# Normalization and output products moved from VectorE to GpSimd in pieces placed under PSUM reads, with six more VectorE tiles

## The chip, the cores and the metric

One core of a Trainium2 chip runs the kernel; seven are idle. The metric is the device time of one execution in microseconds (us). A kernel's time is the median of its runs.

## The reference, cut to what matters

```python
B, H, S, D = 1, 32, 2048, 640;  Dh = D // H            # 20 columns per head
def reference(q, k, v, t):
    eps = 1e-6
    qn = q / (jnp.sqrt((q * q).sum(axis=-1, keepdims=True)) + eps)
    kn = k / (jnp.sqrt((k * k).sum(axis=-1, keepdims=True)) + eps)
    logits = jnp.einsum('bhqd,bhkd->bhqk', qn, kn) * t[None, :, None, None]
    attn = _softmax(logits, axis=-1)
    return jnp.einsum('bhqk,bhkd->bhqd', attn, v)
```

This is attention over 32 heads with normalized queries and keys. A head has 2048 x 2048 scores, so 134 million exponentials have to be made. They are the work that two engines share.

## The kernel before

For every head there are 16 key tiles of 128 keys. Each key tile makes 128 x 2048 scores, in four units of 512 columns. A tile goes one of two ways.

- **ScalarE tiles**: ScalarE reads two or three units of scores from PSUM and writes their exponentials to a ring in SBUF.
- **VectorE tiles**: VectorE reads the scores from PSUM in two halves of 1024 columns and writes `score * X_MUL + X_ADD` as int16. Read as fp16 bits, that is a rough power of two. Three "phase adds" then make shifted copies in SBUF. TensorE multiplies the four versions by scaled copies of `v` (the "value matmuls"; those that make the scores are the "score matmuls"), and the sum is a good exponential. So one VectorE tile costs two PSUM reads and three phase adds.

`MORE` sets how many heads get a fifth VectorE tile: there are `4 * 32 + MORE` of them, 139 in the kernel before.

```python
    MORE = 11
    DVE_TILES = [4 + (h * MORE // 31 > (h - 1) * MORE // 31 if h else 0) for h in range(H)]
    ...
    # PSUM read, two of them per tile
    e.tensor_scalar(xt[sx][:, o:o + W1], psD[:, slot * W1:slot * W1 + W1], X_MUL, X_ADD, ALU.mult, ALU.add)
    # phase add, three per tile
    e.tensor_scalar(ss[i][se][:, 0:w], x, float(PHASES[i]), None, ALU.add)
```

Besides that, VectorE makes the squared sums and the reciprocal roots, and two products with a broadcast factor. The change moves most of both.

```python
                # normalization product, once per head: 2 * 16 * 20 = 640 elements per partition
                norm[h] = dv("norm", lambda e, tk, x=x, b=b, i=i: e.tensor_tensor(
                    qkn[b][:, :, 0:D], x[:, :, :], bc(rs["r"][:, 2 * R * i:2 * R * (i + 1)], 2 * R), ALU.mult),
                    0.735, [c] + war)
    ...
            # output product, once per head: 320 elements
            fin[h] = add("DVE", f"fin{h}", lambda e, tk: e.tensor_tensor(st, src, rb, ALU.mult),
                         0.40, [rc] + (sto[h - 2] if h >= 2 else []), due)
```

GpSimd makes only the scaled copies of `v` (three per head) as soon as `v` has landed. All orders are set on the host by a list scheduler inside the kernel file, which gives each engine a fixed sequence with semaphore waits.

Of the kernel before, what the change touches and what calls it, by code (L numbers as in the profile page):

```python
# [11 lines left out]
F32 = mybir.dt.float32  # L12
I32 = mybir.dt.int32
# [14 lines left out]
class Task:  # L28
    __slots__ = ("eng", "fn", "dur", "deps", "pri", "name", "lat", "dma", "n", "users",
                 "start", "end", "seq", "inc", "cnt", "rows", "work", "modes")  # L30

    def __init__(self, eng, name, fn, dur, deps, pri, lat=0.0, dma=None):
        self.eng, self.name, self.fn, self.dur = eng, name, fn, dur
        self.deps = [d for d in deps if d is not None]
        self.pri, self.lat, self.dma = pri, lat, dma
        self.inc, self.cnt = False, 0
        self.rows, self.work, self.modes = 128, 512.0, None


class Program:  # L40
# [23 lines left out]
    def schedule(self):  # L64
# [29 lines left out]
        self.heavy = heavy  # L94
        return self.order

    def list_schedule(self):
        for t in self.tasks:
            t.users = []
        for i, t in enumerate(self.tasks):  # L100
            t.seq = i
            deps = []
            for d in t.deps:
                deps += d() if callable(d) else [d]
            t.deps = list(dict.fromkeys(deps))
            t.n = len(t.deps)
            for d in t.deps:
                d.users.append(t)
# [22 lines left out]
        order = {e: [] for e in free}  # L131
        done = 0
        last_pe = [""]
        while events:
# [9 lines left out]
            for e in touched:  # L144
                if free[e] > now + 1e-9 or not ready[e]:
                    continue
# [9 lines left out]
                if e == "PE":  # L156
                    x = min(ready[e], key=lambda r: (r[0] + (0.0 if r[2].name[:2] == last_pe[0] else self.SWITCH), r[1]))
                    ready[e].remove(x)
                    heapq.heapify(ready[e])
                    t = x[2]  # L160
                else:
                    _, _, t = heapq.heappop(ready[e])
# [3 lines left out]
                t.end = now + t.dur  # L166
# [12 lines left out]
                for u in t.users:  # L179
                    lat = t.lat if t.dma else (  # L180
                        self.SEM_LAT[e] if u.eng != e else 0.12 if e == "DVE" else 0.0)
                    if u.eng == "PE" and u.name[:2] == "pv":
                        lat += self.PV_SLACK
                    rt[u.seq] = max(rt[u.seq], t.end + lat)
                    u.n -= 1
                    if u.n == 0:
                        arrive(u, rt[u.seq])
# [60 lines left out]
def bass_standalone__qk_norm__prompt_kernel(  # L248
# [32 lines left out]
    MORE = 11  # L281
    DVE_TILES = [4 + (h * MORE // 31 > (h - 1) * MORE // 31 if h else 0) for h in range(H)]
    NDMAX = 5

    with ExitStack() as es:
# [5 lines left out]
        ones = sbuf("ones", [128, 512], BF16)  # L291
        ident = sbuf("ident", [128, 128], BF16)
# [13 lines left out]
        oT = sbuf("oT", [128, R, 32], F32)  # L306
        rec = sbuf("rec", [128, R], F32)
# [12 lines left out]
        def memset(eng, ap, val, dur, pri):  # L320
            return add(eng, "z", lambda e, tk: e.memset(ap, val), dur, pri=pri)
# [36 lines left out]
        z_one = memset("DVE", ones[:, :], 1.0, 0.2, -99)  # L358
        z_id = add("POOL", "id", lambda e, tk: e.affine_select(
# [26 lines left out]
        def add_loads(h):  # L386
            b, bv = h % NB, h % NV
            pri = h - LEAD - 0.5
            war = ([norm[h - NB]] if h >= NB else []) + ([lambda: [trn[max(0, h - 4)]]] if h >= EARLY else [])
# [14 lines left out]
            if h == 1:  # L404
# [6 lines left out]
                0.5, [ld_v[h]] + (pv_users[h - NV] if h >= NV else z_v[bv]), pri + 0.2) for i in range(len(PHASES))]  # L411

        def add_prep(hs):
# [33 lines left out]
            if hs[0] == 0:  # L447
                first_head(c)
                prep_last[0] = [norm[0], head0[-1]]
                return  # L450
            for i, h in enumerate(hs):
                x, b = qk_sb[h % NB], h % NN
                war = [trn[h - NN]] + (q0 if h == NN else []) if h >= NN else [z_qkn[b]]
                norm[h] = dv("norm", lambda e, tk, x=x, b=b, i=i: e.tensor_tensor(  # L454
                    qkn[b][:, :, 0:D], x[:, :, :], bc(rs["r"][:, 2 * R * i:2 * R * (i + 1)], 2 * R), ALU.mult),
                    0.735, [c] + war)
            prep_last[0] = [norm[h] for h in hs]
# [3 lines left out]
        def add_trn(h):  # L461
# [5 lines left out]
                qkn[b][:, :, :].rearrange("p r d -> p (r d)")), 1.3, [norm[h]] + war, due + 0.1, lat=3.0, dma=f"T{bt}")  # L467
# [15 lines left out]
        def first_head(rinv):  # L483
# [46 lines left out]
            norm[0] = nq  # L530
# [43 lines left out]
        def add_fin(h):  # L574
            b2 = h % 2
            due = h + 0.9
            trO[h] = add("DVE", f"tr{h}", lambda e, tk: e.transpose(  # L577
                oT[:, :, :].rearrange("p r d -> p (r d)"), psO[:, :]), 0.63,
                [lambda: pv_users[h]] + ([fin[h - 1]] if h else []), -10 + due)
# [3 lines left out]
            if h == 0:  # L583
# [3 lines left out]
            fin[h] = add("DVE", f"fin{h}", lambda e, tk: e.tensor_tensor(st, src, rb, ALU.mult),  # L587
                         0.40, [rc] + (sto[h - 2] if h >= 2 else []), due)
# [61 lines left out]
        def add_dgroup(jg):  # L650
# [33 lines left out]
            def dv(name, fn, dur, deps):  # L684
                return add("DVE", f"{name}{js[0]}", fn, 0.068 + dur * len(js), deps, due)
            sh = [dv(f"s{i}.", lambda e, tk, i=i: e.tensor_scalar(  # L686
                ss[i][se][:, 0:w], x, float(PHASES[i]), None, ALU.add), 0.533, t1s + old(f"s{i}", NE)) for i in range(len(PHASES))]
            dusers["x", jg] = list(sh)
            for nm, tile, dep, ph in [("x", xt[sx], t1s, None)] + [(f"s{i}", ss[i][se], [sh[i]], i) for i in range(len(PHASES))]:
# [85 lines left out]
```

## Time and profile before

| | before |
|---|---|
| time, median of 3 runs | 700.74 us (699.8 to 700.9) |
| span of the profiled run | 699.4 us |
| VectorE busy | 691.8 us |
| ScalarE busy | 684.3 us |
| GpSimd busy | 41.2 us |

First come two lines of the page of the kernel before: the busy time of each engine with its share of the span and number of instructions (PE is TensorE, PEld its weight loads, DVE VectorE, ACT ScalarE, POOL GpSimd), and the chain of work that ended last, by engine.

```profile
PE 628.4 (90%) x5742; PEld 167.9 (24%) x5792; DVE 691.8 (99%) x1046; ACT 684.3 (98%) x605; POOL 41.2 (6%) x116
...
DVE 65%; ACT 30%; PE 3%; issue 2%; ACTq 0%
```

VectorE and ScalarE are both within 2.2% of the span, and the chain runs now through one and now through the other.

Next are groups of VectorE's instructions in the kernel before, by source line and shape. The columns are line, engine, operation, output<-inputs, shapes, count, then busy time in us and the mean in ns of one, then idle time before them and what ended it.

```profile
L678 DVE TENSOR_SCALAR xt<-psD 128x1024 int16<-128x1024 f32 x278 | 338.3, 1217 | 1.3 <-PE psD L546 1.1
L686 DVE TENSOR_SCALAR ss<-xt 128x2048 int16<-128x2048 int16 x417 | 274.3, 688 | 0.3
...
L454 DVE TENSOR_TENSOR qkn<-qk_sb,rs_r 128x640 bf16<-128x640 bf16 x31 | 24.8, 815 | 0.0
...
L587 DVE TENSOR_TENSOR o_stage<-oT,rec 128x320 bf16<-128x320 f32 x32 | 15.6, 488 | 0.0
```

These are the PSUM reads, the phase adds, the normalization products and the output products. The means slightly overstate the cost, as one instruction overlaps the next by about 0.08 us: from start to start a PSUM read takes 1.134 us, a phase add 0.600, a normalization product 0.735 and an output product 0.40.

The same view for ScalarE's exponentials, of three units and of two:

```profile
L632 ACT ACTIVATE p_ring<-psA 128x1536 bf16<-128x1536 f32 x298 | 459.7, 1543 | 8.1 <-PE psA L546 7.5
L632 ACT ACTIVATE p_ring<-psA 128x1024 bf16<-128x1024 f32 x299 | 335.2, 1121 | 0.6 <-PE psA L546 0.6
```

From start to start they take 1.330 and 0.904 us.

Last, the timeline of one collision (start in us, duration in us, engine, what), VectorE first and GpSimd after it:

```profile
79.51 0.78 DVE L686 TENSOR_SCALAR ss<-xt 128x2048 int16<-128x2048 int16 x1
80.21 1.21 DVE L678 TENSOR_SCALAR xt<-psD 128x1024 int16<-128x1024 f32 x1
```

```profile
79.44 1.37 POOL L409 TENSOR_SCALAR vph<-vaug 128x128 f16<-128x128 bf16 x3 [28.46 <-DMA vaug<-in_v_dram]
```

The phase add at 79.51 took 0.78 us where 0.68 is usual, since a scaling of `v` on GpSimd was running. The PSUM read behind it, with GpSimd still busy until 80.81, kept its usual 1.21. This small difference is what the change builds on.

### The profile page before, as it was taken

The page shows a single profiled execution, that of the slowest core. Times are in us where ns is not written, and L with a number is a line of the kernel's source. Part 1 is how long each engine was busy: PE and PEld are TensorE (multiplying, and loading weights), DVE is VectorE, ACT ScalarE, POOL GpSimd, SP SyncE. Part 2 cuts the span into 40 slices and gives each one's busy share as a digit, 9 for nine tenths or more (in the row PEclk, how much of TensorE's full clock was granted, in tenths as well). Part 3 has the DMA queues.
Part 4 walks back from the last instruction along what each step waited for, and adds up shares of the span by engine and source line. Part 5 has one row for each costly group of instructions (what it writes and reads, how often), then busy time and mean ns, then how long its engine had stood idle before and what let it go on. Part 6 is the DMA issues. An engine that isn't in the chain of part 4 may idle for free.

```text
span 699.4 us, 14049 instructions
## 1 busy us (share of the span) xinstructions
PE 628.4 (90%) x5742; PEld 167.9 (24%) x5792; DVE 691.8 (99%) x1046; ACT 684.3 (98%) x605; POOL 41.2 (6%) x116
## 2 busy tenths in 40 slices
PE   8798888999899898998999999989989989999997
PEld 2222222222222222222222222222222222222221
DVE  9999999999999999999999999999999999999998
ACT  8889999999999999999999999999999999999997
POOL 3110100101001010100101001010010100100000
PEclk9989999999999999999999999999999999999999
DMA  5452403434034342402424024240342514123000
GB/s 64 68 74 63 66 8 76 49 71 58 6 87 44 70 54 55 73 9 66 60 51 76 9 67 59 60 67 8 87 40 56 72 22 85 17 69 61 27 6 10
DMA packets 196720, 36.20 MB, mean 52 GB/s; under 512 B 172592, under 2 KB 196656, under 8 KB 196656
## 3 DMA queue, kind: packets, MB, share of 16 engines
q1 hardware_dynamic: 196512, 35.22, 30.7%
q8 instruction: 45, 0.74, 0.4%
q14 instruction: 19, 0.16, 0.1%
q10 hardware_dynamic: 144, 0.08, 0.0%
HBM read 7.87 MB, written 2.62 MB: 15 GB/s over the span
## 4 chain that ended last, share of the span: by engine, by line
DVE 65%; ACT 30%; PE 3%; issue 2%; ACTq 0%
DVE xt L678 30%; ACT p_ring L632 30%; DVE ss L686 22%; DVE rs_sum L428 2%; DVE qkn L454 2%; DVE oT L577 2%; DVE sq L426 1%; DVE o_stage L587 1%; PE psA L546 1%; PE psO L565 1%; PE psD L546 1%; DVE rs_b L438 1%; DVE rs_a L436 1%; DVE rec L580 0%; DVE rs_r L440 0%
## 5 line engine op out<-in xcount | busy, mean ns | idle before, releaser
L632 ACT ACTIVATE p_ring<-psA 128x1024 bf16<-128x1024 f32 x597 | 677.6, 1332 | 8.8 <-PE psA L546 8.1
L678 DVE TENSOR_SCALAR xt<-psD 128x1024 int16<-128x1024 f32 x278 | 338.3, 1217 | 1.3 <-PE psD L546 1.1
L546 PE MATMUL psA<-qz,kR 64*128 64x512 bf16 (+2 forms) x1092 | 247.4, 385 | 30.9 <-ACT p_ring L632 25.3
L686 DVE TENSOR_SCALAR ss<-xt 128x2048 int16<-128x2048 int16 x417 | 274.3, 688 | 0.3
L565 PE MATMUL psO<-ss,vph 128*32 128x512 f16 x1668 | 155.4, 385 | 0.2
L565 PE MATMUL psO<-p_ring,vaug 128*32 128x512 bf16 x1492 | 138.6, 385 | 0.4 <-ACT p_ring L632 0.2
L546 PE MATMUL psA<-qz,qkT 64*128 64x512 bf16 (+2 forms) x370 | 123.9, 385 | 9.1 <-ACT p_ring L632 6.0
L546 PE MATMUL psD<-qz,kR 64*128 64x512 bf16 (+1 forms) x402 | 114.2, 387 | 19.7 <-DVE xt L678 11.1
L546 PEld LDWEIGHTS psA<-qz,kR 32*128 32x128 bf16 (+2 forms) x1119 | 58.5, 93 | 178.6 <-ACT p_ring L632 161.0
L409 POOL TENSOR_SCALAR vph<-vaug 128x128 f16<-128x128 bf16 (+1 forms) x96 | 38.0, 395 | 596.5 <-DMA vaug<-in_v_dram 591.1
L565 PEld LDWEIGHTS psO<-ss,vph 128*32 128x32 f16 x1668 | 39.3, 94 | 78.4 <-issue 49.8
L546 PE MATMUL psD<-qz,qkT 64*128 64x512 bf16 (+1 forms) x134 | 51.1, 385 | 5.2 <-DVE xt L678 4.0
L565 PE MATMUL psO<-xt,vaug 128*32 128x512 f16 x556 | 53.8, 388 | 0.1
L565 PEld LDWEIGHTS psO<-p_ring,vaug 128*32 128x32 bf16 x1492 | 36.4, 94 | 62.7 <-issue 55.0
L546 PEld LDWEIGHTS psD<-qz,kR 64*128 64x128 bf16 (+1 forms) x417 | 28.0, 94 | 83.3 <-DVE xt L678 74.7
L546 PEld LDWEIGHTS psA<-qz,qkT 64*128 64x128 bf16 (+2 forms) x373 | 29.9, 93 | 59.1 <-ACT p_ring L632 53.9
L428 DVE TENSOR_REDUCE rs_sum<-sq 128x32 f32<-128x640 bf16 x32 | 26.0, 813 | 0.5
L454 DVE TENSOR_TENSOR qkn<-qk_sb,rs_r 128x640 bf16<-128x640 bf16 x31 | 24.8, 815 | 0.0
L577 DVE STREAM_TRANSPOSE oT<-psO 128x512 f32<-128x512 f32 x32 | 22.7, 709 | 1.2 <-PE psO L565 1.2
L565 PEld LDWEIGHTS psO<-xt,vaug 128*32 128x32 bf16 x556 | 13.8, 94 | 31.5 <-issue 20.4
L546 PEld LDWEIGHTS psD<-qz,qkT 64*128 64x128 bf16 (+1 forms) x139 | 12.9, 94 | 28.0 <-DVE xt L678 21.4
L426 DVE TENSOR_TENSOR sq<-qk_sb 128x640 bf16<-128x640 bf16 x32 | 15.7, 490 | 0.1
(40 smaller groups left out, 80.2 us busy)
## 6 DMA issues: line engine op xcount, KB each, us to landing
kR<-qkT SPq DMA_DIRECT2D x62, 96.0 KB, 2.1
qz<-qkT SPq DMA_DIRECT2D x124, 32.0 KB, 1.9
kR<-qkT SPq DMA_DIRECT2D x62, 64.0 KB, 2.0
qk_sb<-in_k_dram SPq DMA_DIRECT2D x32, 80.0 KB, 2.4
vaug<-in_v_dram SPq DMA_DIRECT2D x32, 80.0 KB, 3.3
qk_sb<-in_q_dram SPq DMA_DIRECT2D x124, 20.0 KB, 2.5
out_dram<-o_stage SPq DMA_DIRECT2D x31, 80.0 KB, 2.0
kR<-qkT SPq DMA_DIRECT2D x62, 32.0 KB, 1.9
```

The costliest lines, as they stand in the source:

```text
L409: vsc[h] = [add("POOL", f"vs{h}", lambda e, tk, i=i: e.tensor_scalar(vph[bv][:, i, 0:nd, :], vaug[bv][:, R - nd:R, :], 2.0 ** (-PHASES[i] ...
L426: s1 = dv("sq", lambda e, tk, x=x: e.tensor_tensor(sq[:, :, :], x[:, :, :], x[:, :, :], ALU.mult), 0.41, lds[h] + last_sum + (q0[2:] if h ...
L428: sums.append(dv("sum", lambda e, tk, i=i: e.tensor_reduce(rs["sum"][:, 2 * R * i:2 * R * (i + 1)], sq[:, :, :], AXIS_X, ALU.add), 0.73, [ ...
L436: c = dv("rs", lambda e, tk, cur=cur: e.tensor_tensor(rs["a"][:, 0:w], cur[:, 0:w], cur[:, 0:w], ALU.mult), 0.07 + 0.03 * n, [c])
L438: c = dv("rs", lambda e, tk: e.scalar_tensor_tensor(rs["b"][:, 0:w], rs["a"][:, 0:w], -0.5, rs["sum"][:, 0:w], ALU.mult, ALU.mult), 0.07 + ...
L454: norm[h] = dv("norm", lambda e, tk, x=x, b=b, i=i: e.tensor_tensor(qkn[b][:, :, 0:D], x[:, :, :], bc(rs["r"][:, 2 * R * i:2 * R * (i + 1) ...
L546: return eng.matmul(dst, lhsT, mov, tile_position=(p0, 0))
L565: last = eng.matmul(psO[32 * g:32 * g + 32, :], w, rhs_of(g), start=start, stop=False, skip_group_check=True, tile_position=(0, 32 * g))
L577: trO[h] = add("DVE", f"tr{h}", lambda e, tk: e.transpose(oT[:, :, :].rearrange("p r d -> p (r d)"), psO[:, :]), 0.63, [lambda: pv_users[h ...
L632: act[w] = add("ACT", f"exp{w}", lambda e, tk: e.activation(p_ring[:, p0 * 512:p0 * 512 + n], psA[:, slot * WAVES[0] * 512:slot * WAVES[0] ...
L678: t1_prev[nchunk[0]] = add("DVE", f"t1.{j}.{k}", lambda e, tk, o=o, slot=slot: e.tensor_scalar(xt[sx][:, o:o + W1], psD[:, slot * W1:slot ...
L686: sh = [dv(f"s{i}.", lambda e, tk, i=i: e.tensor_scalar(ss[i][se][:, 0:w], x, float(PHASES[i]), None, ALU.add), 0.533, t1s + old(f"s{i}", ...
```

## The change

The intent is to take 29 of the 32 normalization products and 30 of the 32 output products off VectorE, where these cost 33 us, to let GpSimd do them while VectorE reads PSUM, and to spend the time won on six more VectorE tiles, so that ScalarE gets less too. The normalization is split in two pieces of 320 elements; the output product has 320 anyway. Four of the 435 phase adds go to GpSimd as well, as int32 additions in three pieces (352, 352 and 320).

```diff
-    MORE = 11
+    MORE = 17
-    NDMAX = 5
+    NDMAX = 6
+    NPOOL, FPOOL = True, True
+    TTDUR, TTWIN = 0.95, 0.9
+    KDN = (0,) * 29 + (1,)
+    PCH, PRATE = 352, 0.0022
...
+                if NPOOL and h > 2:
+                    for j in range(2):
+                        u = add("POOL", f"norm{h}", lambda e, tk, x=x, b=b, i=i, j=j: e.tensor_tensor(
+                            qkn[b][:, R * j:R * (j + 1), 0:D], x[:, R * j:R * (j + 1), :],
+                            bc(rs["r"][:, 2 * R * i + R * j:2 * R * i + R * (j + 1)], R), ALU.mult),
+                            TTDUR, [c] + war, due + SPREAD)
+                        u.win = TTWIN
...
+            pool = FPOOL and 0 < h < H - 1
+            fin[h] = add("POOL" if pool else "DVE", ...)
...
+        oTs = [sbuf(f"oT{i}", [128, R, 32], F32) for i in range(2)]     # was one buffer
```

`KDN` says which tiles give one phase add to GpSimd (one tile in 30), `TTDUR` how long the scheduler takes a product on GpSimd to be, and `TTWIN` how much room it must have.

The scheduler learns where to put pieces with a window (`win`). When it starts a PSUM read, a transpose or a squared sum on VectorE, it fills that stretch with ready GpSimd pieces. Each gets one more dependency, its trigger, which is the VectorE instruction in front of the read, or the one before that when a phase add stands between:

```diff
+        def pool_fill(now):
+                s = max(now, free["POOL"], span[0])
+                fit = [r for r in ready["POOL"] if r[2].win and s + r[2].win <= span[1]]
...
+                d = order["DVE"]
+                i = len(d) - 2
+                if i > 0 and d[i].start - d[i - 1].end < 0.02 and d[i].name[0] == "s" and d[i + 1].start - d[i].end < 0.02:
+                    i -= 1
+                t.trig = d[i] if i >= 0 else None
...
+        for t in self.tasks:
+            if t.trig is not None:
+                t.deps.append(t.trig)
```

The scalings of `v` get windows too.

More of the change, by code (lines that the diff above doesn't have):

```diff
@@ L29 @@
     __slots__ = ("eng", "fn", "dur", "deps", "pri", "name", "lat", "dma", "n", "users",
-                 "start", "end", "seq", "inc", "cnt", "rows", "work", "modes")
+                 "start", "end", "seq", "inc", "cnt", "rows", "work", "modes", "win", "trig")
     def __init__(self, eng, name, fn, dur, deps, pri, lat=0.0, dma=None):
@@ L37, in __init__ @@
         self.rows, self.work, self.modes = 128, 512.0, None
+        self.win, self.trig = 0.0, None
 class Program:
@@ L99, in list_schedule @@
             t.users = []
+            t.trig = None
         for i, t in enumerate(self.tasks):
@@ L131, in list_schedule, with leave @@
         order = {e: [] for e in free}
+        span = [0.0, 0.0]
+        def leave(t, now):
+            for u in t.users:
+                lat = t.lat if t.dma else (
+                    self.SEM_LAT[t.eng] if u.eng != t.eng else 0.12 if t.eng == "DVE" else 0.0)
+                if u.eng == "PE" and u.name[:2] == "pv":
+                    lat += self.PV_SLACK
+                rt[u.seq] = max(rt[u.seq], t.end + lat)
+                u.n -= 1
+                if u.n == 0:
+                    arrive(u, max(now, rt[u.seq]))
+        def pool_fill(now):
+            n = 0
+            while True:
+                s = max(now, free["POOL"], span[0])
+                fit = [r for r in ready["POOL"] if r[2].win and s + r[2].win <= span[1]]
+                if not fit:
+                    return n
+                x = min(fit)
+                ready["POOL"].remove(x)
+                heapq.heapify(ready["POOL"])
+                t = x[2]
+                d = order["DVE"]
[3 more added lines that the diff above has]
+                t.trig = d[i] if i >= 0 else None
+                t.start, t.end = s, s + t.dur
+                free["POOL"] = t.end
+                lock[0] = s + t.win
+                order["POOL"].append(t)
+                heapq.heappush(events, (t.end, 1, t.seq, t))
+                leave(t, now)
+                n += 1
+        lock = [0.0]
         done = 0
         last_pe = [""]
-        while events:
+        while events or ready["POOL"]:
+            if not events:
+                now = max(free.values())
+                span[:] = [now, now + 9.0]
+                done += pool_fill(now)
             now = events[0][0]
@@ L144, in list_schedule @@
             for e in touched:
-                if free[e] > now + 1e-9 or not ready[e]:
+                if e == "POOL":
+                    done += pool_fill(now)
+                if free[e] > now + 1e-9 or not ready[e] or e == "POOL" and all(r[2].win for r in ready[e]):
                     continue
@@ L160, in list_schedule @@
                     t = x[2]
+                elif e == "POOL":
+                    x = min(r for r in ready[e] if not r[2].win)
+                    ready[e].remove(x)
+                    heapq.heapify(ready[e])
+                    t = x[2]
                 else:
@@ L165, in list_schedule @@
                 t.start = now
-                t.end = now + t.dur
+                if e == "DVE":
+                    if t.name[:2] in ("t1", "tr", "su"):
+                        span[:] = [now, now + t.dur]
+                    else:
+                        t.start = max(now, lock[0])
+                t.end = t.start + t.dur
                 if e == "PE":
@@ L178, in list_schedule @@
                 heapq.heappush(events, (t.end, 1, t.seq, t))
-                for u in t.users:
-                    lat = t.lat if t.dma else (
-                        self.SEM_LAT[e] if u.eng != e else 0.12 if e == "DVE" else 0.0)
-                    if u.eng == "PE" and u.name[:2] == "pv":
-                        lat += self.PV_SLACK
-                    rt[u.seq] = max(rt[u.seq], t.end + lat)
-                    u.n -= 1
-                    if u.n == 0:
-                        arrive(u, rt[u.seq])
+                leave(t, now)
+                if e == "DVE" and span[0] == t.start:
+                    done += pool_fill(now)
         assert done == len(self.tasks), "dependence cycle"
@@ L291, in bass_standalone__qk_norm__prompt_kernel @@
         ones = sbuf("ones", [128, 512], BF16)
+        two = sbuf("two", [128, 1], I32)
         ident = sbuf("ident", [128, 128], BF16)
@@ L305, in bass_standalone__qk_norm__prompt_kernel @@
         ss = [[sbuf(f"ss{j}_{i}", [128, GD * 2048], I16) for i in range(NE)] for j in range(len(PHASES))]
-        oT = sbuf("oT", [128, R, 32], F32)
-        rec = sbuf("rec", [128, R], F32)
+        oTs = [sbuf(f"oT{i}", [128, R, 32], F32) for i in range(2)]
+        recs = [sbuf(f"rec{i}", [128, R], F32) for i in range(2)]
         o_stage = [sbuf(f"o_stage{i}", [128, R * D], BF16) for i in range(2)]
@@ L358, in bass_standalone__qk_norm__prompt_kernel @@
         z_one = memset("DVE", ones[:, :], 1.0, 0.2, -99)
+        memset("POOL", two[:, :].bitcast(I16), PHASES[2], 0.1, -98)
         z_id = add("POOL", "id", lambda e, tk: e.affine_select(
@@ L388, in add_loads @@
             pri = h - LEAD - 0.5
-            war = ([norm[h - NB]] if h >= NB else []) + ([lambda: [trn[max(0, h - 4)]]] if h >= EARLY else [])
+            war = (norm[h - NB] if h >= NB else []) + ([lambda: [trn[max(0, h - 4)]]] if h >= EARLY else [])
             x = qk_sb[b]
@@ L410, in add_loads @@
                 vph[bv][:, i, 0:nd, :], vaug[bv][:, R - nd:R, :], 2.0 ** (-PHASES[i] / 1024.0), 1.0, ALU.mult, ALU.mult),
-                0.5, [ld_v[h]] + (pv_users[h - NV] if h >= NV else z_v[bv]), pri + 0.2) for i in range(len(PHASES))]
+                0.4, [ld_v[h]] + (pv_users[h - NV] if h >= NV else z_v[bv]), pri + 0.2) for i in range(len(PHASES))]
+            for u in vsc[h] if h else []:
+                u.win = 0.36
         def add_prep(hs):
@@ L448, in add_prep @@
                 first_head(c)
-                prep_last[0] = [norm[0], head0[-1]]
+                prep_last[0] = norm[0] + head0[-1:]
                 return
@@ L453, in add_prep @@
                 war = [trn[h - NN]] + (q0 if h == NN else []) if h >= NN else [z_qkn[b]]
-                norm[h] = dv("norm", lambda e, tk, x=x, b=b, i=i: e.tensor_tensor(
-                    qkn[b][:, :, 0:D], x[:, :, :], bc(rs["r"][:, 2 * R * i:2 * R * (i + 1)], 2 * R), ALU.mult),
-                    0.735, [c] + war)
-            prep_last[0] = [norm[h] for h in hs]
+                if NPOOL and h > 2:
+                    norm[h] = []
+                    for j in range(2):
[4 more added lines that the diff above has]
+                        u.win = TTWIN
+                        norm[h].append(u)
+                else:
+                    norm[h] = [dv("norm", lambda e, tk, x=x, b=b, i=i: e.tensor_tensor(
+                        qkn[b][:, :, 0:D], x[:, :, :], bc(rs["r"][:, 2 * R * i:2 * R * (i + 1)], 2 * R), ALU.mult),
+                        0.735, [c] + war)]
+            prep_last[0] = [u for h in hs for u in norm[h]]
             for h in hs:
@@ L466, in add_trn @@
                 qkT[bt][:, :].rearrange("p (c n) -> p c n", n=128),
-                qkn[b][:, :, :].rearrange("p r d -> p (r d)")), 1.3, [norm[h]] + war, due + 0.1, lat=3.0, dma=f"T{bt}")
+                qkn[b][:, :, :].rearrange("p r d -> p (r d)")), 1.3, norm[h] + war, due + 0.1, lat=3.0, dma=f"T{bt}")
             rot[h] = [dma("SP", f"qz{h}", qz[bt][32 * g:32 * g + 32, g, :], qkT[bt][32 * g:32 * g + 32, 0:512],
@@ L529, in first_head @@
                 cp[2 * dl - 2:2 * dl], -20, lat=2.5, dma=f"R0{dl}") for dl in range(1, 4)]
-            norm[0] = nq
+            norm[0] = [nq]
             head0.append(nk)
@@ L576, in add_fin @@
             due = h + 0.9
+            oT, rec = oTs[b2], recs[b2]
             trO[h] = add("DVE", f"tr{h}", lambda e, tk: e.transpose(
                 oT[:, :, :].rearrange("p r d -> p (r d)"), psO[:, :]), 0.63,
-                [lambda: pv_users[h]] + ([fin[h - 1]] if h else []), -10 + due)
+                [lambda: pv_users[h]] + ([fin[h - 2]] if h > 1 else []), -10 + due)
             rc = add("DVE", f"rec{h}", lambda e, tk: e.reciprocal(rec[:, :], oT[:, :, D]), 0.165, [trO[h]], due)
@@ L586, in add_fin @@
                 rb = bass.AP(rec, 0, [rec[:, :].ap[0], [4, 4], [1, 4], [0, D]])
-            fin[h] = add("DVE", f"fin{h}", lambda e, tk: e.tensor_tensor(st, src, rb, ALU.mult),
-                         0.40, [rc] + (sto[h - 2] if h >= 2 else []), due)
+            pool = FPOOL and 0 < h < H - 1
+            fin[h] = add("POOL" if pool else "DVE", f"fin{h}", lambda e, tk: e.tensor_tensor(st, src, rb, ALU.mult),
+                         TTDUR if pool else 0.40, [rc] + (sto[h - 2] if h >= 2 else []), due)
+            if pool:
+                fin[h].win = TTWIN
             if h == 0:
@@ L685, in dv @@
                 return add("DVE", f"{name}{js[0]}", fn, 0.068 + dur * len(js), deps, due)
-            sh = [dv(f"s{i}.", lambda e, tk, i=i: e.tensor_scalar(
-                ss[i][se][:, 0:w], x, float(PHASES[i]), None, ALU.add), 0.533, t1s + old(f"s{i}", NE)) for i in range(len(PHASES))]
-            dusers["x", jg] = list(sh)
-            for nm, tile, dep, ph in [("x", xt[sx], t1s, None)] + [(f"s{i}", ss[i][se], [sh[i]], i) for i in range(len(PHASES))]:
+            sh = []
+            for i in range(len(PHASES)):
+                dst, war = ss[i][se], t1s + old(f"s{i}", NE)
+                if i < 2 or jg < 2 or KDN[jg % len(KDN)] == 0:
+                    sh.append([dv(f"s{i}.", lambda e, tk, i=i, dst=dst: e.tensor_scalar(
+                        dst[:, 0:w], x, float(PHASES[i]), None, ALU.add), 0.533, war)])
+                    continue
+                sh.append([])
+                for c in range(0, w // 2, PCH):
+                    n = min(PCH, w // 2 - c)
+                    u = add("POOL", f"s{i}.{js[0]}.{c}", lambda e, tk, i=i, dst=dst, c=c, n=n: e.tensor_tensor(
+                        dst[:, 2 * c:2 * (c + n)].bitcast(I32), xt[sx][:, 2 * c:2 * (c + n)].bitcast(I32),
+                        bass.AP(two, 0, [two[:, :].ap[0], [0, n]]), ALU.add), 0.25 + n * PRATE, war, due)
+                    u.win = 0.2 + n * PRATE
+                    sh[-1].append(u)
+            dusers["x", jg] = [u for us in sh for u in us]
+            for nm, tile, dep, ph in [("x", xt[sx], t1s, None)] + [(f"s{i}", ss[i][se], sh[i], i) for i in range(len(PHASES))]:
                 us = dusers.setdefault((nm, jg), [])
```

## The prediction

> **What bounds the kernel now.** Two engines together. The page gives VectorE 691.8 us busy of a 699.4 us span (99%) and ScalarE 684.3 us (98%). The chain of waits is 65% VectorE, 30% ScalarE, 3% TensorE. The waits view shows ScalarE losing only 8.1 us to TensorE (one wait of 3.9 us near 36 us), and VectorE about 2.5 us. GpSimd is 6% busy. So time falls only if VectorE and ScalarE both get less work, and then by the smaller cut.
>
> **Costs, as start-to-start distances on the timeline** (neighbours overlap by about 0.08 us): PSUM read of 1024 columns 1.134 us; phase add of 2048 int16 0.600; normalization product 0.735; output product 0.40; exponentials 0.904 (two units) and 1.330 (three), mean 1.117.
>
> **VectorE.** Removed: 29 normalization products (21.3 us), 30 output products (12.0), four phase adds done by GpSimd in three chunks each (2.4): 35.7 us. Added: MORE 11 to 17 gives six more VectorE tiles, each two PSUM reads and three phase adds, 4.07 us: 24.4 us. Net -11.3 us.
>
> **ScalarE.** Six tiles less are 24 units, 9.6 exponentials: -10.7 us. The cuts are balanced. TensorE gets 18 more groups of four value matmuls and slightly fewer score waves, about 4 us, which its slack should absorb.
>
> **Does GpSimd's work cost VectorE anything?** The Trainium skill, "SBUF — State Buffer", section "Who interferes with whom", says VectorE and GpSimd share one port pair as an exclusive lock: a VectorE instruction in a 2-port mode or with two SBUF inputs excludes GpSimd's, one outside these doesn't. The trace agrees: PSUM reads that overlap today's value scalings keep 1.134 us (33 of them), while overlapped phase adds go from 0.601 to 0.65 in the median and 0.73 at the ninth decile. The change starts almost every GpSimd piece so that it runs under a PSUM read: in the instruction order it is released by the VectorE instruction one or two before a PSUM read, often with one phase add between, which should hold the lock until the read starts. The skill's "GPSIMD Engine Reference", section 3.1, gives about 2.6 cycles per element for two inputs; for 320 elements at 1.2 GHz that is an estimate of 0.69 us, plus a dispatch of perhaps 0.2: about 0.9 us, under 1.134. No run yet shows this duration. I expect spills of under 0.1 us on a minority of the 100 large pieces (+1 to +2 us in all), and about 1.5 us won because value scalings no longer collide with phase adds. The order up to head 2 is unchanged, so the start-up stall stays. The moved products' latency is hidden: normalization runs three heads ahead.
>
> **Predicted time: 690 us (-1.5%), range 686 to 696.** Chances: faster by over 2% (below 686.7) 0.13, within 2% 0.82, slower 0.05.
>
> **What would show each step.** VectorE busy falls to about 680 us, ScalarE's to about 674, both still 98 to 99%. 290 PSUM reads, 431 phase adds, 587 exponentials. GpSimd busy rises by about 90 us, to about 130. Its 320-element products last 0.8 to 1.0 us (longer where they first wait behind a phase add). PSUM reads and phase adds keep 1.217 and about 0.68 us. The granted clock stays at 0.99.
>
> **What would make it wrong.** GpSimd products longer than about 1.1 us would run into the next phase add or two-input VectorE instruction; 100 pieces with 0.3 us each would give back 30 us and make the kernel slower. A late release would put pieces under phase adds. If ScalarE's present waits grow because VectorE's tiles or TensorE's extra groups bunch, the gain shrinks to 5 us. If collisions today cost more than I read, it could pass 2%.

## The result, and the profile after

| | before | after |
|---|---|---|
| time, median of 4 runs each | 700.82 us | 691.09 us (690.8 to 692.01) |
| ratio, with 95% interval | | 0.9865 (0.9848 to 0.9882) |
| VectorE busy | 691.8 us | 678.9 us |
| ScalarE busy | 684.3 us | 674.5 us |
| GpSimd busy | 41.2 us | 149.5 us |
| granted TensorE clock | 0.994 | 0.997 |

The change is 1.35% faster, which is less than 2% and clear of noise.

The same two lines of the page, of the changed kernel:

```profile
PE 630.3 (91%) x5806; PEld 168.8 (24%) x5864; DVE 678.9 (98%) x1013; ACT 674.5 (98%) x596; POOL 149.5 (22%) x217
...
DVE 61%; ACT 28%; PE 7%; issue 1%; DMA 1%; SPq 1%; DVEq 0%
```

Both busy times fell, by 12.9 and 9.8 us, and the two engines are as full as before. Groups of VectorE's instructions, then ScalarE's exponentials, then GpSimd's products, by line and shape:

```profile
L754 DVE TENSOR_SCALAR xt<-psD 128x1024 int16<-128x1024 f32 x290 | 352.0, 1214 | 4.0 <-PE psD L618 3.7
L766 DVE TENSOR_SCALAR ss<-xt 128x2048 int16<-128x2048 int16 x431 | 281.7, 681 | 0.3
```

```profile
L708 ACT ACTIVATE p_ring<-psA 128x1536 bf16<-128x1536 f32 x293 | 445.4, 1520 | 7.8 <-PE psA L618 6.3
L708 ACT ACTIVATE p_ring<-psA 128x1024 bf16<-128x1024 f32 x294 | 322.6, 1097 | 0.8 <-PE psA L618 0.8
...
L708 ACT ACTIVATE p_ring<-psA 128x512 bf16<-128x512 f32 x1 | 0.7, 721 | 0.0
```

```profile
L519 POOL TENSOR_TENSOR qkn<-qk_sb,rs_r 128x320 bf16<-128x320 bf16 x58 | 61.7, 1065 | 81.1 <-DVE ss L766 52.6 <-DVE oT L650 16.8 <-DVE rs_r L508 8.0
L661 POOL TENSOR_TENSOR o_stage<-oT,rec 128x320 bf16<-128x320 f32 x30 | 30.1, 1002 | 204.4 <-DVE rec L653 65.2 <-DVE ss L766 48.8 <-DVE rs_r L508 39.0
```

There are 12 more PSUM reads (290), 14 more phase adds (431) and 9 fewer exponentials (588, one of them of a single unit). From start to start each kind takes what it took before (medians of 1.134 and 0.602 us, and 1.331 and 0.904 us). GpSimd's products seem to take 1.0 to 1.1 us. The timeline shows why that is not their cost. VectorE, then GpSimd, in one stretch of the changed kernel:

```profile
305.41 1.30 DVE L766 TENSOR_SCALAR ss<-xt 128x2048 int16<-128x2048 int16 x2
306.62 1.22 DVE L754 TENSOR_SCALAR xt<-psD 128x1024 int16<-128x1024 f32 x1
307.75 0.69 DVE L766 TENSOR_SCALAR ss<-xt 128x2048 int16<-128x2048 int16 x1
308.36 1.23 DVE L754 TENSOR_SCALAR xt<-psD 128x1024 int16<-128x1024 f32 x1
309.62 1.30 DVE L766 TENSOR_SCALAR ss<-xt 128x2048 int16<-128x2048 int16 x2
```

```profile
306.18 1.11 POOL L519 TENSOR_TENSOR qkn<-qk_sb,rs_r 128x320 bf16<-128x320 bf16 x1 [1.35 <-DVE ss L766]
308.52 0.73 POOL L519 TENSOR_TENSOR qkn<-qk_sb,rs_r 128x320 bf16<-128x320 bf16 x1 [1.23 <-DVE ss L766]
```

The piece at 308.52 was released just behind the start of the PSUM read at 308.36 and took 0.73 us. The piece at 306.18 was released while the second of two phase adds ran, and its record of 1.11 us holds a wait: it ended at 307.29, so with 0.73 us of work it began at 306.56, which is about where the read begins (306.62). Either way it was over before the next phase add (307.75 and 309.62). VectorE shows no trace of it. The trace has 75 of the 88 products recorded like the first, from within a phase add, and all 75 end 0.47 to 0.67 us after the start of their read.

### The profile page after: what moved, and what is told of

It reads as the page before. It is cut to its first block, busy times and chain, and to the rows that moved or that the text cites. A ratio compares the mean times of both kernels' runs of the same rounds, so it can differ in the third digit from the quotient of the medians.

```text
span 689.4 us, 14243 instructions
## 1 busy us (share of the span) xinstructions
PE 630.3 (91%) x5806; PEld 168.8 (24%) x5864; DVE 678.9 (98%) x1013; ACT 674.5 (98%) x596; POOL 149.5 (22%) x217
## 4 chain that ended last, share of the span: by engine, by line
DVE 61%; ACT 28%; PE 7%; issue 1%; DMA 1%; SPq 1%; DVEq 0%
DVE xt L754 31%; ACT p_ring L708 28%; DVE ss L766 23%; PE psO L637 3%; PE psA L618 2%; DVE oT L650 2%; DVE rs_sum L490 2%; PE psD L618 1%; DVE sq L488 1%; SPq L377 1%; DMA qkT<-qkn 1%; DVE rs_b L500 0%; DVE rec L653 0%; DVE rs_a L498 0%; DMA qk_sb<-in_k_dram 0%
## 5 line engine op out<-in xcount | busy, mean ns | idle before, releaser
L708 ACT ACTIVATE p_ring<-psA 128x1024 bf16<-128x1024 f32 x588 | 667.7, 1307 | 8.5 <-PE psA L618 7.1
L754 DVE TENSOR_SCALAR xt<-psD 128x1024 int16<-128x1024 f32 x290 | 352.0, 1214 | 4.0 <-PE psD L618 3.7
L766 DVE TENSOR_SCALAR ss<-xt 128x2048 int16<-128x2048 int16 x431 | 281.7, 681 | 0.3
L637 PE MATMUL psO<-ss,vph 128*32 128x512 f16 x1740 | 159.1, 386 | 0.4
L637 PE MATMUL psO<-p_ring,vaug 128*32 128x512 bf16 x1468 | 134.8, 385 | 0.0
L618 PEld LDWEIGHTS psA<-qz,kR 64*128 64x128 bf16 (+2 forms) x1101 | 57.2, 93 | 162.9 <-ACT p_ring L708 150.0
L469 POOL TENSOR_SCALAR vph<-vaug 128x160 f16<-128x160 bf16 (+2 forms) x96 | 41.7, 434 | 211.6 <-DMA vaug<-in_v_dram 99.7
L519 POOL TENSOR_TENSOR qkn<-qk_sb,rs_r 128x320 bf16<-128x320 bf16 x58 | 61.7, 1065 | 81.1 <-DVE ss L766 52.6
L661 POOL TENSOR_TENSOR o_stage<-oT,rec 128x320 bf16<-128x320 f32 x30 | 30.1, 1002 | 204.4 <-DVE rec L653 65.2
L637 PE MATMUL psO<-xt,vaug 128*32 128x512 f16 x580 | 57.5, 386 | 0.1
```

Of the source, the lines that this page charges most:

```text
L469: vsc[h] = [add("POOL", f"vs{h}", lambda e, tk, i=i: e.tensor_scalar(vph[bv][:, i, 0:nd, :], vaug[bv][:, R - nd:R, :], 2.0 ** (-PHASES[i] ...
L519: u = add("POOL", f"norm{h}", lambda e, tk, x=x, b=b, i=i, j=j: e.tensor_tensor(qkn[b][:, R * j:R * (j + 1), 0:D], x[:, R * j:R * (j + 1), :],
L618: return eng.matmul(dst, lhsT, mov, tile_position=(p0, 0))
L637: last = eng.matmul(psO[32 * g:32 * g + 32, :], w, rhs_of(g), start=start, stop=False, skip_group_check=True, tile_position=(0, 32 * g))
L661: fin[h] = add("POOL" if pool else "DVE", f"fin{h}", lambda e, tk: e.tensor_tensor(st, src, rb, ALU.mult), TTDUR if pool else 0.40, [rc] + ...
L708: act[w] = add("ACT", f"exp{w}", lambda e, tk: e.activation(p_ring[:, p0 * 512:p0 * 512 + n], psA[:, slot * WAVES[0] * 512:slot * WAVES[0] ...
```

## The experiments

The kernel before ran on the same chip in the same rounds; ratios are against that. Only e4 and e5 keep the changed kernel's order on VectorE and GpSimd; in all others the scheduler sets the orders anew.

### e1: the products moved, without more tiles

```diff
-    MORE = 17
+    MORE = 11
```

> GpSimd products kept, but MORE back at 11, so ScalarE keeps its 597 exponentials. My theory (both engines bind, the smaller cut counts): VectorE busy falls to about 654 us, ScalarE's stays near 684, time 697 to 701 us, and VectorE's idle time grows to over 40 us. Rival (VectorE alone binds, the tiles are a side matter): time falls by about the 35.7 us taken off VectorE, to about 666 us.

Measured: 700.2 us, ratio 0.9996 (0.9981 to 1.0011). The page, and from the waits view VectorE's longest wait (who waited for whom, us in total, times, longest):

```profile
PE 630.1 (90%) x5739; PEld 171.2 (24%) x5792; DVE 661.9 (95%) x983; ACT 683.6 (98%) x605; POOL 145.9 (21%) x217
```

```profile
DVE oT L650 <- PE psO L637: 17.6, 6, 10.2
```

VectorE had 29.9 us less to do than before and time did not move. ScalarE kept its work, and the page's chain runs through it for 69%. VectorE stood idle for 37 us (span 698.9 less 661.9; I had expected over 40) and at the end waited 10.2 us for the last value matmuls. Its busy time is some 7 us above my figure of 654. Most of that is overlap lost at idle gaps: 147 of its instructions start after their predecessor's end, against 69 before, and 78 times 0.08 us is 6 us. The rival that VectorE alone binds is out.

### e2: the tiles added, with all products left on VectorE

```diff
-    NPOOL, FPOOL = True, True
+    NPOOL, FPOOL = False, False
-    KDN = (0,) * 29 + (1,)
+    KDN = (0,)
```

> MORE 17, but all products and phase adds stay on VectorE. My theory: VectorE binds with 24.4 us more work; VectorE busy about 715 us, ScalarE about 674, time 719 to 726 us. Rival (ScalarE is what binds, its 10 us less is the whole gain): about 690 us.

Measured: 719.6 us, ratio 1.0273 (1.0256 to 1.0290).

```profile
PE 636.5 (89%) x5809; PEld 169.8 (24%) x5864; DVE 711.5 (99%) x1076; ACT 675.8 (94%) x596; POOL 40.8 (6%) x117
```

ScalarE's work fell by 8.5 us and time rose by 19, within my forecast, as VectorE was full. The rival that ScalarE's relief is the whole gain is out.

### e3: neither

```diff
-    MORE = 17
+    MORE = 11
-    NPOOL, FPOOL = True, True
+    NPOOL, FPOOL = False, False
-    KDN = (0,) * 29 + (1,)
+    KDN = (0,)
```

> MORE 11 and all products on VectorE; what is left of the change is the double-buffered transposed output and the placement of the value scalings under PSUM reads. My theory: 699 to 701 us, at most 1.5 us below the kernel before (the 24 phase adds that ran slower beside a value scaling). Rival (the gain comes from the buffers or from the scalings' placement): about 691 us.

Measured: 699.49 us, ratio 0.9987 (0.9973 to 1.0002). VectorE was busy for 690.0 us against 691.8. The second transposed buffer and the placing of the scalings of `v` are worth at most a microsecond or two, and as the interval includes 1, no gain in time is shown. The rival is out.

The four corners together (us):

| | products on VectorE | products on GpSimd |
|---|---|---|
| 139 VectorE tiles | 699.5 (e3) | 700.2 (e1) |
| 145 VectorE tiles | 719.6 (e2) | 691.1 (the change) |

Moving the products does nothing by itself, adding tiles costs 20 us by itself, and both together win 8.4 (9.7 against the kernel before).

### e4: the pieces released as soon as their data are there

The order of instructions on each engine is the same as in the changed kernel; only the trigger is left out.

```diff
-            if t.trig is not None:
-                t.deps.append(t.trig)
+            pass
```

> The changed kernel with the same order on every engine, but GpSimd's pieces are no longer held back for a PSUM read: each starts when its data are there. Theory of the shared port pair: pieces fall under phase adds and the products with two inputs, phase adds that meet a product stretch from 0.60 us to as much as 1.3, VectorE busy rises by 8 to 25 us, time 694 to 710 us. Rival (placement does not matter, GpSimd's work is free anywhere): phase adds keep 0.60 us, time 690 to 692 us.

Measured: 714.04 us, ratio 1.0198 (1.0183 to 1.0213), 23 us above the changed kernel's 691.09. Groups of PSUM reads and phase adds:

```profile
L753 DVE TENSOR_SCALAR xt<-psD 128x1024 int16<-128x1024 f32 x290 | 350.9, 1210 | 3.5 <-PE psD L617 3.2
L765 DVE TENSOR_SCALAR ss<-xt 128x2048 int16<-128x2048 int16 x431 | 302.5, 728 | 0.3
```

The PSUM reads kept their length. The page gives the busy times:

```profile
PE 631.9 (89%) x5806; PEld 168.3 (24%) x5864; DVE 702.1 (99%) x1013; ACT 681.2 (96%) x596; POOL 143.3 (20%) x217
```

The phase adds grew from 281.7 to 302.5 us busy, and VectorE's busy time from 678.9 to 702.1, by 23.2 us, which is the loss of time. One place, VectorE and then GpSimd:

```profile
315.70 0.17 DVE L507 TENSOR_TENSOR rs_r<-rs_r,t_f 128x32 f32<-128x32 f32 x1
315.81 1.83 DVE L765 TENSOR_SCALAR ss<-xt 128x2048 int16<-128x2048 int16 x2
317.56 1.21 DVE L753 TENSOR_SCALAR xt<-psD 128x1024 int16<-128x1024 f32 x1
```

```profile
315.95 4.08 POOL L518 TENSOR_TENSOR qkn<-qk_sb,rs_r 128x320 bf16<-128x320 bf16 x4 [9.07 <-DVE rs_r L507]
```

Two phase adds took 1.83 us instead of 1.28, with four normalization pieces queued up next to them. VectorE's rise lies within what I expected, but my range of 694 to 710 for the time was too low at its upper end: all of the rise became time.

### e5: the pieces released one instruction later

Each piece with a trigger waits for the end of the read (or of the transpose or sum) that it was meant to run under. The second edit only keeps the scheduler's bookkeeping in order.

```diff
-                t.trig = d[i] if i >= 0 else None
+                t.trig = d[-1] if i >= 0 else None
...
                 t.deps.append(t.trig)
+                t.start = max(t.start, t.trig.start + 1e-6)
```

> The changed kernel, but each GpSimd piece that was released just before a PSUM read is released by the end of that read, one instruction later, so that it meets the phase adds behind the read. Theory of the shared port pair: the phase add under way makes the piece wait, then the piece takes the pair and the next phase add waits up to 0.7 us; some 60 of the 100 large pieces cost about 0.55 us each, phase adds total 25 to 45 us more, time 715 to 735 us, worse than free release. Rival (what hurt in free release was that pieces ran back to back, not where they fell): time near 691, at most 697 us.

Measured: 733.32 us, ratio 1.0475 (1.0460 to 1.0491), 42 us above the changed kernel. Here the pieces are spread out as in the change: no large piece follows another within 0.15 us, which happens 56 times in e4. So bunching is not needed for the loss; what it added in e4 is not separated. The page, the groups, then one place on VectorE and on GpSimd:

```profile
PE 644.0 (88%) x5864; PEld 167.8 (23%) x5864; DVE 721.3 (99%) x1013; ACT 684.4 (94%) x596; POOL 162.2 (22%) x217
```

```profile
L755 DVE TENSOR_SCALAR xt<-psD 128x1024 int16<-128x1024 f32 x290 | 351.3, 1211 | 2.8 <-PE psD L619 2.4
L767 DVE TENSOR_SCALAR ss<-xt 128x2048 int16<-128x2048 int16 x431 | 318.6, 766 | 0.3
```

```profile
311.59 0.68 DVE L767 TENSOR_SCALAR ss<-xt 128x2048 int16<-128x2048 int16 x1
312.19 0.80 DVE L503 SCALAR_TENSOR_TENSOR rs_y<-rs_b,rs_u 128x64 f32<-128x64 f32 x1
312.90 0.24 DVE L654 RECIPROCAL rec<-oT 128x16 f32<-128x16 f32 x1
```

```profile
311.75 1.14 POOL L773 TENSOR_TENSOR ss<-xt,two 128x352 int32<-128x352 int32 x1 [5.50 <-DVE xt L755]
```

The piece was released at 311.75, when a phase add had just begun, and ended at 312.89. Such a piece takes 0.77 us where it waits for nothing, so it began at about 312.12, near the end of the phase add. The small two-input instruction at 312.19, which elsewhere takes 0.22, took 0.80, and the next one on VectorE started at 312.90, when the piece was done. The same trace shows what a piece does not touch: 15 transposes and 11 squared sums that overlap a piece's record by over 0.3 us kept 0.631 and 0.73 us, while five squares that overlap one, instructions with two inputs, took 0.83 us on average instead of 0.40. Phase adds rose by 36.9 us to 318.6. VectorE's busy time was 721.3 us, 42.4 us more than in the changed kernel, and again that is the whole loss.

### e6: normalization in one piece of 640

```diff
-                    for j in range(2):
+                    for j in range(1):
...
-                            qkn[b][:, R * j:R * (j + 1), 0:D], x[:, R * j:R * (j + 1), :], ..., TTDUR, ...)
+                            qkn[b][:, :, 0:D], x[:, :, :], ..., 1.65, ...)
```

> Each normalization on GpSimd in one piece of 640 elements instead of two of 320, still released for a PSUM read. From the free pieces of the changed kernel (0.715 us for 320 and 0.772 for 352 int32 elements, 0.727 for 320 bf16) I estimate 1.3 to 1.4 us for 640. Theory: it outlasts the read of 1.134 us by 0.2 to 0.4 us, most of the 29 pieces hold up the next phase add by that, phase adds gain 4 to 9 us in total, time 694 to 699 us. Rival (only the start of a piece matters, or the read's length is no limit): 690 to 692 us.

Measured: 691.07 us, ratio 0.9872 (0.9857 to 0.9887), the same as the change. This expectation failed. VectorE, then GpSimd:

```profile
306.10 1.30 DVE L766 TENSOR_SCALAR ss<-xt 128x2048 int16<-128x2048 int16 x2
307.31 1.22 DVE L754 TENSOR_SCALAR xt<-psD 128x1024 int16<-128x1024 f32 x1
308.44 0.69 DVE L766 TENSOR_SCALAR ss<-xt 128x2048 int16<-128x2048 int16 x1
```

```profile
306.87 1.65 POOL L519 TENSOR_TENSOR qkn<-qk_sb,rs_r 128x640 bf16<-128x640 bf16 x1 [1.35 <-DVE ss L766]
```

The shortest of the 640-element pieces took 1.27 us. That makes this one, which ended at 308.52, begin at about 307.25, near the start of the read (307.31). (The 0.715 us in my expectation is from e4's trace, not from the changed kernel's.) Its end lay 0.08 us behind the start of the next phase add, which still took 0.69 us. 23 of the 29 pieces are released early enough to begin with the read, so 1.27 us still fits a read of 1.134 us. Of the other six, two start while VectorE stands idle before its read, and four some 0.15 us into their read; the phase add or square behind these four stretched by 0.05 to 0.2 us. The size of 320 is not needed here.

### e9: two pieces under one read

```diff
-    TTDUR, TTWIN = 0.95, 0.9
+    TTDUR, TTWIN = 0.5, 0.55
-                    if t.name[:2] in ("t1", "tr", "su"):
+                    if t.name[:2] == "t1":
```

> Both 320-element halves of a normalization back to back under one PSUM read, the second released by nothing but the first (29 pairs). The single piece of 640 lasted 1.27 us and its end lay about 0.08 us behind the reported start of the next VectorE instruction without slowing it. Two halves take about 0.73 + 0.70 = 1.43 us, so the end should lie some 0.25 us behind that start. Theory of the lock: about 20 of the 29 pairs are followed by a phase add or a two-input instruction and cost it 0.15 to 0.3 us, 3 to 7 us in all, time 692 to 698 us. Rival (a spill costs nothing, GpSimd's later accesses slip between): 690 to 691.5 us.

Measured: 692.94 us, ratio 0.9896 (0.9879 to 0.9914). The phase adds were busy for 283.9 us against 281.7, and the longest lasted 0.97 us from start to start where none of the changed kernel passed 0.74. That one, on VectorE and then GpSimd:

```profile
637.06 1.15 DVE L754 TENSOR_SCALAR xt<-psD 128x1024 int16<-128x1024 f32 x1
638.14 1.65 DVE L766 TENSOR_SCALAR ss<-xt 128x2048 int16<-128x2048 int16 x2
```

```profile
637.22 1.41 POOL L519 TENSOR_TENSOR qkn<-qk_sb,rs_r 128x320 bf16<-128x320 bf16 x2 [11.32 <-DVE rec L653]
```

The two halves end at 638.63, 0.49 us behind the start of the phase add, and that phase add is 0.36 us longer than usual. The traces of e6 and e9 together show how a spill is paid. A piece that ends 0.07 to 0.08 us behind the recorded start of a phase add costs it nothing (14 cases in e6); 0.18 us costs 0.05 and 0.30 us costs 0.17 (e6); 0.21 to 0.22 us costs 0.08 to 0.09 (21 cases in e9); 0.49 us costs 0.36. So the phase add is longer by the spill less 0.13 us, each time to about 0.01 us. The rival is out: a spill is paid in full beyond the first 0.13 us. Why the first 0.13 us are free is not shown. A pair that spilled onto a phase add mostly cost 0.09 us, and not the 0.15 to 0.3 us that I expected. The whole time shows little of this: 2.2 us more of phase adds is less than the 3 to 7 us I expected, VectorE's busy time in all is 678.8 us against 678.9, and VectorE waited 6.3 us for the last value matmuls instead of 1.2.

### e7 and e8: more phase adds on GpSimd

```diff
-    KDN = (0,) * 29 + (1,)
+    KDN = (0,) * 3 + (1,)        # e7; e8: (0,) * 7 + (1,)
-    MORE = 17
+    MORE = 20                    # e7; e8: 19
```

> One phase add in four tiles on GpSimd in three pieces (36 instead of 4) and MORE 20 instead of 17. By the same sum as for the change: VectorE loses 32 adds of 0.60 us and gains three tiles of 4.07, -7.0 us; ScalarE loses 4.8 exponentials, -5.4 us. If there are reads enough (about 293 PSUM reads for 196 large pieces and the scalings): 685 to 687 us. If pieces come too late for TensorE or crowd under phase adds: 690 us or more.

> One phase add in eight tiles on GpSimd (18 instead of 4) and MORE 19. Sum: VectorE loses 14 adds and gains two tiles, -0.3 us; ScalarE loses 3.2 exponentials, -3.6 us. VectorE then binds: 689.5 to 691.5 us, the same as the changed kernel; if time falls by 3 us or more, ScalarE binds more than I think.

Measured: e7 705.96 us, ratio 1.0083 (1.0068 to 1.0099); e8 720.52 us, ratio 1.0297 (1.0280 to 1.0314). Both sums failed (e7 fell under its second case, "690 us or more"), although the phase adds were no longer than before. In e7 VectorE and ScalarE stood still for 5.4 and 7.3 us near 590 us, waiting for score matmuls, which waited for rotated keys (copies of a head's keys that DMAs make once they are normalized and transposed): the normalization of that head had been placed only three PSUM reads before the head's own first one. In e8 the two longest of VectorE's waits, near 600 us, were these:

```profile
DVE sq L488 <- DMA qk_sb<-in_q_dram: 11.4, 2, 11.0
...
DVE ss L766 <- PE psO L637: 7.3, 1, 7.3
```

The square waited for a load of `q` that stood in the one DMA-issuing queue behind two transposes and some twenty copies; the transposes waited for GpSimd's products. VectorE's order is fixed, and it ran nothing from 588.06 to 599.03.

The stalls have a sequel. Two rows of the view by windows in e8, before and after the first stall (window and its length, busy time and count of TensorE, weight loads, VectorE, ScalarE and GpSimd, then the granted TensorE clock, the DMA share and GB/s):

```profile
580.00:590.00 10.00, 8.41 (x81) 2.21 (x75) 7.72 (x18) 9.84 (x10) 2.77 (x5) 1.00 0.60 90
600.00:610.00 10.00, 7.74 (x25) 1.00 (x23) 2.40 (x3) 5.89 (x5) 2.90 (x5) 0.50 0.26 55
```

VectorE fell idle at 588.06, and the granted clock was 0.50 from 595.0 to 615.4; the second wait, for value matmuls, lies in that stretch. In e7 the clock was 0.50 from 589.8 to 596.7, again after VectorE had fallen idle. So a stall here was followed by a stretch at half the clock. How much of the lost time is due to that was not separated.

### e10: e7 with normalization due half a head earlier

```diff
-    LEAD = 3.0
+    LEAD = 3.5
```

> The kernel of e7 (36 phase adds on GpSimd, MORE 20) with its normalizations due half a head earlier (LEAD 3.5 instead of 3.0). In e7's order the products of one head end only 3 PSUM reads before the head's own first read, here never under 10. If late products are why e7 took 706 us: its stalls of 5 and 7 us near 590 us vanish and the time is 685 to 688 us. If e7 was slow because GpSimd's pieces crowd VectorE, it stays above 697 us.

Measured: 696.61 us, ratio 0.9942 (0.9927 to 0.9957). The stall near 590 us is gone, as expected, and VectorE has no idle gap above 1 us before the end. The time lies between the two cases that I had named. ScalarE waited 10.8 us in eight places for value matmuls to free its ring, and VectorE waited 9.0 us at the end for the last ones. So the earlier normalization won 9 us back, and something else keeps this kernel from its sum.

### e11: e10 with normalization in one piece

```diff
-                    for j in range(2):
+                    for j in range(1):
...
-                            qkn[b][:, R * j:R * (j + 1), 0:D], x[:, R * j:R * (j + 1), :], ..., TTDUR, ...)
+                            qkn[b][:, :, 0:D], x[:, :, :], ..., 1.35, ...)
```

> The same with each normalization in one piece of 640, which e6 showed to cost VectorE nothing and which leaves 29 PSUM reads to other pieces. Same sums: 684.5 to 688 us; below e10 by up to 1 us if free reads are what limits e10, equal otherwise.

Measured: 687.34 us, ratio 0.9812 (0.9798 to 0.9827). This is within the expected range and the fastest kernel. It is 1.9% faster than the kernel before (the interval straddles 2%) and 3.7 us below the change. But it is 9.3 us below e10, where I expected at most 1, so the freed reads as I reckoned them don't explain the difference.

```profile
PE 636.3 (93%) x5900; PEld 168.4 (25%) x5900; DVE 672.9 (98%) x995; ACT 667.7 (97%) x591; POOL 230.4 (34%) x287
```

VectorE and ScalarE have 6.0 and 6.8 us less to do than in the changed kernel, close to the sums of 7.0 and 5.4.

### e12: e10 with fewer 128-row score matmuls

```diff
-    LOAD = 3500.0
+    LOAD = 3300.0
```

`LOAD` is the least matmul work that the scheduler wants in any 3.41 us of TensorE's order. Where there is less, it gives score matmuls the 128-row form, which it counts as more work: the "filler".

> The kernel of e10 with the scheduler's target for TensorE's filler (LOAD) lowered from 3500 to 3300, so that 439 instead of 567 score matmuls take the 128-row form (e11 has 421). If e10 was slow because TensorE fell behind (658.6 us busy against 636.3 in e11, VectorE waiting 9.0 us for the last value product): TensorE busy about 640 us, the last wait under 4 us, time 686 to 690 us. If it was the 29 additional GpSimd pieces: unchanged, 695 to 698 us.

Measured: 709.62 us, ratio 1.0134 (1.0109 to 1.0159). TensorE's busy time did fall, to 626.9 us, and the time rose. So my reading of e10, that TensorE had too much work, is wrong or at least not enough. A square on VectorE waited 12.7 us for a load of `q` until 120 us, as in e8, the granted clock was 0.50 from 112.7 to 126.4, and ScalarE waited 25.4 us for value matmuls in the whole run. Which detail of the order decides between e10, e11 and e12 stays open: e11 frees 29 PSUM reads, and it also gets another order on every engine.

## Why the prediction was right

- **What binds.** "Two engines together" is shown by the four corners of e1 to e3: each half of the change alone is worth nothing or costs 20 us.
- **The sizes.** VectorE's cut was predicted as 11.3 us, with 1.5 us more won at the scalings and 1 to 2 us lost to spills, and 12.9 was measured: the moved products took away 33.2 us, the reads added 13.8 and the phase adds 7.0 (8.4 at the predicted 0.600 each), and the rest fell by 0.5. ScalarE's cut was predicted as 10.7 us, and 9.8 was measured. The counts of 290 and 431 came out as said; there are 588 exponentials instead of 587. Time fell by 9.7 us, about the smaller cut, to 691.09 us against 690 predicted. Part of that closeness is luck: the spills did not come, while VectorE's idle time, span less busy, rose from 7.6 to 10.5 us, which the prediction did not have. The 1.1 us that are left are as much as the runs spread (1.2 us) and are not explained.
- **GpSimd's work is free under a PSUM read, a transpose or a squared sum, and not under a phase add or a two-input instruction.** e4 and e5 show it: the same pieces in the same order cost 23 us without their triggers and 42 us when released one instruction late, and VectorE's busy time grew by just these amounts. The section "Who interferes with whom" of the Trainium skill's "SBUF — State Buffer" describes this lock, and the traces agree in direction: PSUM reads kept 1.21 us in all of them, while phase adds rose from 0.681 us in the mean to 0.728 and 0.766, and a two-input instruction from 0.22 to 0.80.
- **The duration of a piece.** I estimated 0.9 us, 0.69 of them from the skill's figure per element, and 0.73 us was measured. The 0.2 us for dispatch had no working in the prediction, but the trace before gives about as much: scalings of 128 and 160 elements took 0.297 and 0.323 us at the least, which by a straight line leaves an estimate of 0.19 us at zero elements. Too large was the term per element (see the last section). The predicted spill of 1 to 2 us in all didn't occur (two phase adds are 0.13 us longer than usual): the phase adds of the changed kernel take 0.599 us from start to start in the mean, against 0.602 before.
- **The scalings of v.** The predicted gain of 1.5 us agrees with VectorE's busy time in e3 (1.8 us less) and with the phase adds of the change (1.4 us less than 14 more of them should bring), but e3's interval of time includes no gain at all. As a gain in time it is not shown.
- **GpSimd's busy time** was predicted near 130 us and is 149.5. The term that was left out is the wait of a piece behind a phase add, about 0.38 us (1.106 in the median, less 0.727), which the record of the piece includes.
- **The start-up stall** stayed, as predicted: ScalarE waited 3.9 us near 36 us before and 4.9 after.

## What to carry to other kernels

When two engines are full, move work off one only together with a shift between the two, and reckon with the smaller of the two cuts. Elementwise work on GpSimd can be free beside VectorE if each piece is released by the instruction in front of one that doesn't use the shared port pair; released when its data happen to be ready, it can cost more than it saves. A piece may outlast that instruction a little: here 0.13 us of spill cost nothing, and the rest was paid in full. Before such pieces are made more numerous, check how early their results are needed: in e8 one late load held VectorE for 11.0 us, and a stretch of 20 us at a granted clock of 0.50 followed.

## What the Trainium skill lacked or had wrong

- "GPSIMD Engine Reference", section 3.1, gives about 2.6 cycles per element for a product of two inputs. Here 320 elements (bf16 times fp32 broadcast) took 0.727 us and 640 took 1.268. The difference is 1.69 ns per element, or 2.0 cycles at the page's 1.2 GHz, and some 0.19 us per instruction remain. With that remainder counted in, 320 elements come to 2.7 cycles each, so the page's figure (0.69 us) is near for this size; the page's own measurement is of fp32 at 2048 elements, a case that no run here has.
- "Perfetto Trace Analysis", section "Optimizing Scalar/DVE Operations", warns that moving work between VectorE and GpSimd might not help, as they share a port. It lacks what placement is worth: the products, the 12 add pieces and the 96 scalings of `v` cost VectorE nothing that shows when placed under PSUM reads, 23 us when started freely (e4) and 42 us when started one instruction late (e5).
- The same page, section "GPSIMD Engine Instruction", calls their recorded spans unreliable without a number. Here products of 0.73 us of work stand in the profile with 1.11 us when they are released during a phase add: the record includes the wait for the port pair.
- "SBUF — State Buffer", section "Who interferes with whom", has no number for how exactly the lock shows in a profile. Here a phase add is longer by the time that a GpSimd piece ends behind its recorded start, less 0.13 us (e6 and e9).
